# Gate and up projections of a SwiGLU layer in seven block products instead of eight

## The chip, the core and the metric

The kernel runs on one core of a Trainium2 chip. The measure is device microseconds of one execution, lower is better. The kernel before was timed three times: 1968.71, 1971.62 and 1972.38 us, with a median of 1971.62 us.

Five engines work side by side: TensorE (PE) multiplies, VectorE (DVE), ScalarE (ACT) and GpSimd (POOL) do elementwise work, and SyncE (SP) issues most of the transfers between main memory and on-chip memory (SBUF). PE writes only into PSUM, an accumulator memory that is used here as eight banks of 128 x 512 floats. Each engine works its instructions in a fixed order and waits at an instruction until what it needs is there.

## The reference

Two layers, each an attention block A and then a feed-forward block B, over 2048 rows of width 512, all in float32. The change touches only B:

```python
x = x + _A_ref(_layernorm(x), ...)
x = x + _B_ref(_layernorm(x), B_w_gate, B_w_up, B_w_down)
...
def _B_ref(x, w_gate, w_up, w_down):      # 512 x 1792, 512 x 1792, 1792 x 512
    g = _silu(x @ w_gate)
    u = x @ w_up
    return (g * u) @ w_down
```

A is causal attention of 32 heads of 16 in four segments of 512 rows, with a running memory (M, z) that is carried from segment to segment, and an output projection.

## The kernel before

**Precision by splitting.** Every float32 operand of a projection is split into a high part in PE's faster format (an ACT copy that rounds) and a low part, the rest (a subtraction on DVE, in attention partly on POOL). A product is three groups of matmuls: high x high, low x high, high x low. So one 512-deep product of a 128 x 512 tile is 3 x 4 = 12 matmuls with 512 columns each, and a 256-deep one is 6.

**The feed-forward stage** (`ffn`, line 799). The 1792 hidden columns are cut into 7 chunks of 256 (`NF`), the rows into 4 blocks of 512. A loop over chunks holds a loop over the blocks. For a chunk and a block, `up` (line 846) makes two halves of 128 columns; each is a gate product and an up product of 12 matmuls into their own banks (line 856), a silu on ACT (line 865), the product of both on DVE (line 866), and the split into high and low h (lines 868 and 869). `down` (line 874) then makes four products of 6 matmuls with `w_down` (line 883), and DVE adds each to the block's running result in SBUF (line 888). Weights are fetched once per chunk by `load_gu` and `load_d`; `load_part` (line 808) copies the high part on ACT (814) and makes the low part on DVE (815). All four blocks' normed and transposed rows stay in SBUF for the whole stage (buffers `H0` to `H3`, `L0` to `L3`).

**What sets the order.** The kernel records all operations with a priority and a cost, and `Program.issue` (line 144) then lays them out: it walks an own model of the engines' time and gives each engine, whenever it is free, the ready operation of lowest priority number. Each engine's instruction order is fixed by that. Priorities are places on a time line, `base + v * T`: in the feed-forward stage v counts blocks. `EARLY_AT` lets the first two blocks of chunk 0 start inside attention's last segment.

**Buffers.** Big tiles take named slots (`ffn_slots`, `att1`, `att2`); a new tile in a slot waits for all operations of the one before. The PSUM banks are `plt_0` to `plt_2`, `ppv`, `pmx_0`, `pmx_1` and two `pj`. `up` takes the first four in turn, `down` the `pmx` and `pj` banks.

## Time and profile before

| | before |
|---|---|
| median of three runs | 1971.62 us |
| profiled execution: time, span | 1972.77 us, 1971.0 us |
| PE busy in the span, matmuls | 1925.4 us, 11392 |
| DVE, ACT, POOL busy | 1145.0, 733.3, 474.0 us |
| PE's granted clock | 0.997 of full |

The profile is one execution. A busy time is the sum of an engine's instructions; PE's is of overlapping, pipelined matmuls. A group of instructions is given by line, engine, operation and tiles, with its count, its busy time, the mean of one, and after the bar the engine's idle time just before it and what ended that. A window row gives the same for a stretch of the span. Line numbers are those of the kernel before; tile names `s` are SBUF slots.

### The profile page before, as it was taken

To read this page: it belongs to the slowest core of one execution; us is meant where nothing else is said; L and a number is where in the kernel's file an instruction comes from. 1 tells how busy PE (TensorE), PEld (TensorE's weight loads), DVE (VectorE), ACT (ScalarE), POOL (GpSimd) and SP (SyncE) were. 2 spreads that over 40 slices of the span, in tenths; PEclk is the share of its full clock that TensorE was granted. 3 is DMA by queue.
4 is the path that set the end of the run, shared out by engine and by line. 5 is a ranking of instruction groups with operands and counts; after the bars stand their busy time and mean duration, and the time that the engine had idled before them with its cause. 6 is when DMAs were issued, how large, how long until landed. Compare 5 with 4: busy or idle time off the path is not lost.

```text
span 1971.0 us, 31446 instructions
## 1 busy us (share of the span) xinstructions
PE 1925.4 (98%) x11392; PEld 1493.2 (76%) x11392; DVE 1145.0 (58%) x3446; ACT 733.3 (37%) x1374; POOL 474.0 (24%) x731
## 2 busy tenths in 40 slices
PE   7999999999999999999999999999989999999999
PEld 5677677776778888888877777777767788888887
DVE  5877777778653333333558777776885433333333
ACT  4555554545521221121235545454554221211211
POOL 5333444434310000000333344343343000000000
PEclk9999999999999999999999999999999999999999
DMA  7444434456230100010364344453552201100002
GB/s 236 130 114 129 125 118 146 132 153 194 81 107 12 32 22 27 16 33 22 102 203 114 114 143 116 119 156 119 177 156 98 74 12 32 33 22 11 17 1 86
DMA packets 101547, 184.01 MB, mean 93 GB/s; under 512 B 12816, under 2 KB 28176, under 8 KB 101392
## 3 DMA queue, kind: packets, MB, share of 16 engines
q1 hardware_dynamic: 99344, 181.47, 30.2%
q8 instruction: 91, 1.49, 0.3%
q10 hardware_dynamic: 2048, 0.53, 0.1%
q14 instruction: 64, 0.52, 0.1%
HBM read 114.32 MB, written 67.11 MB: 92 GB/s over the span
## 4 chain that ended last, share of the span: by engine, by line
PE 89%; DVE 3%; DMA 3%; ACT 2%; issue 1%; POOL 1%; SPq 0%; ACTq 0%; DVEq 0%; POOLq 0%
PE plt L856 22%; PE pj L278 16%; PE pmx L527 8%; PE pj L883 8%; PE pmx L883 8%; PE ppv L856 7%; PE ppv L599 7%; PE plt L571 6%; PE pj L856 2%; DVE junk L534 1%; DMA s<-nm 1%; DMA ck<-scrk 1%; PE pj L369 1%; PE pmx L278 1%; PE pj L649 1%
## 5 line engine op out<-in xcount | busy, mean ns | idle before, releaser
L856 PE MATMUL plt<-s,s 128*128 128x512 f32 x1872 | 536.6, 393 | 0.0
L534 DVE CUSTOM_DVE_ANT_0 junk<-pmx,amask 128x128 bf16<-128x128 f32 (+3 forms) x1024 | 458.5, 484 | 128.1 <-PE pmx L527 123.4
L278 PE MATMUL pj<-s,s 128*128 128x512 f32 x1416 | 476.6, 409 | 0.3
L856 PEld LDWEIGHTS plt<-s,s 128*128 128x128 f32 x1872 | 351.1, 188 | 79.6 <-issue 0.8
L577 ACT ACTIVATE s<-plt 128x512 f32<-128x512 f32 x512 | 284.3, 600 | 156.1 <-PE plt L571 139.5
L527 PE MATMUL pmx<-ck,s 127*128 127x256 f32 (+2 forms) x1024 | 301.7, 349 | 17.1 <-DVE mx L534 10.8
L278 PEld LDWEIGHTS pj<-s,s 128*128 128x128 f32 x1416 | 263.0, 190 | 65.4 <-issue 24.5
L571 PE MATMUL plt<-s,ck 128*128 128x256 f32 x1280 | 242.7, 289 | 7.6 <-DMA s<-nm 6.2
L527 PEld LDWEIGHTS pmx<-ck,s 127*128 127x128 f32 x1024 | 179.5, 190 | 91.8 <-DVE mx L534 29.0
L856 PE MATMUL ppv<-s,s 128*128 128x512 f32 x624 | 243.9, 392 | 0.0
L571 PEld LDWEIGHTS plt<-s,ck 128*128 128x128 f32 x1280 | 214.0, 191 | 35.2 <-DMA s<-nm 7.9
L883 PE MATMUL pj<-s,vt 128*128 128x512 f32 x696 | 177.0, 393 | 0.0
L581 POOL TENSOR_SCALAR_AFFINE_SELECT s<-s 128x512 f32<-128x512 f32 x192 | 127.2, 665 | 194.9 <-ACT s L577 180.4
L865 ACT ACTIVATE Y<-plt 128x512 f32<-128x512 f32 x52 | 31.1, 598 | 370.8 <-PE plt L856 370.8
L883 PE MATMUL pmx<-s,vt 128*128 128x512 f32 x648 | 161.3, 394 | 1.0 <-ACT vt L868 1.0
L866 DVE TENSOR_TENSOR Y<-Y,plt 128x512 f32<-128x512 f32 x52 | 35.7, 687 | 214.6 <-ACT Y L865 214.6
L883 PEld LDWEIGHTS pj<-s,vt 128*128 128x128 f32 x696 | 130.8, 188 | 30.1 <-DVE s L374 0.3
L883 PEld LDWEIGHTS pmx<-s,vt 128*128 128x128 f32 x648 | 121.6, 188 | 29.4 <-ACT vt L868 1.5
L856 PEld LDWEIGHTS ppv<-s,s 128*128 128x128 f32 x624 | 117.1, 188 | 26.5
L599 PE MATMUL ppv<-s,vt 128*32 128x512 f32 (+2 forms) x1536 | 136.8, 458 | 0.0
L866 DVE TENSOR_TENSOR raw<-raw,ppv 128x512 f32<-128x512 f32 x52 | 35.7, 687 | 170.4 <-ACT raw L865 169.6
L351 POOL TENSOR_SCALAR bmv<-bmv 128x1 f32<-128x1 f32 x64 | 16.7, 263 | 490.2 <-DVE bmv L350 486.2
(130 smaller groups left out, 2087.4 us busy)
## 6 DMA issues: line engine op xcount, KB each, us to landing
s<-scrq SPq DMA_DIRECT2D x128, 192.0 KB, 3.5
ck<-scrk SPq DMA_DIRECT2D x128, 192.0 KB, 4.4
scrq<-s SPq DMA_DIRECT2D x32, 512.0 KB, 2.9
scrk<-s SPq DMA_DIRECT2D x32, 512.0 KB, 3.2
scrq<-s SPq DMA_DIRECT2D x32, 256.0 KB, 2.0
scrk<-s SPq DMA_DIRECT2D x32, 256.0 KB, 2.0
xin<-xmid SPq DMA_DIRECT2D x32, 256.0 KB, 2.7
s<-xmid SPq DMA_DIRECT2D x32, 256.0 KB, 4.7
```

The costliest lines, as they stand in the source:

```text
L278: pe(n, passes, lambda: nc.tensor.matmul(view(ps.ap), lhsT=av(a.ap), rhs=bv(b.ap), start=start, stop=stop), [(a, rk[0]), (b, rk[1])], [ps])
L369: pe(128, 2, lambda kc=kc: nc.tensor.transpose(ps.ap[:, kc * 128:(kc + 1) * 128], xn.ap[:, kc * 128:(kc + 1) * 128], ident.ap), [xn, ident ...
L527: nc.tensor.matmul(ps.ap[:, a * 256:a * 256 + nk], lhsT=cq.ap[0:127, 2 * j + p, qt * 128:(qt + 1) * 128], rhs=ck.ap[0:127, p, 0:nk], start ...
L534: dve(w, lambda a=a, qt=qt, w=w, ps=ps, junk=junk: nc.vector.tensor_tensor_reduce(out=junk.ap[:, :w], in0=ps.ap[:, a * 256:a * 256 + w], i ...
L571: nc.tensor.matmul(ps.ap[:, 256 * p:256 * p + 256], lhsT=ck.ap[:, p, kt * 128:kt * 128 + 128], rhs=cq.ap.rearrange("r (j p) c -> r p j c", ...
L577: act(512, lambda: nc.scalar.activation(Pb.ap[:, x].rearrange("p i c -> p (i c)"), ps.ap, AF.Exp, scale=SCALE), [ps], [(Pb, x)], table="exp")
L581: gp(0.593, lambda: nc.gpsimd.affine_select(out=Pb.ap[:, x], in_=Pb.ap[:, x], pattern=[[0, 4], [1, 128]], compare_op=OP.is_ge, fill=0.0, b ...
L599: nc.tensor.matmul(ps.ap[32 * i:32 * i + 32, q0:q0 + w], lhsT=vt.ap[:, kt, VW * hd:VW * hd + 32], rhs=f_[sl].ap[:, b0:b0 + w // 128, idx], ...
L856: pe(512, 1, lambda i=i, j=j, kc=kc, x=x, ps=ps, wt=wt: nc.tensor.matmul(ps.ap, lhsT=wt.ap[:, i, kc, cs], rhs=XT[b][j].ap[:, :, kc], start ...
L865: act(512, lambda: nc.scalar.activation(sg.ap, pg.ap, AF.Silu), [pg], [sg], table="silu")
L866: dve(512, lambda: nc.vector.tensor_mul(sg.ap, sg.ap, pu.ap), [sg, pu], [sg])
L883: pe(512, 1, lambda i=i, j=j, fi=fi, x=x, ps=ps, wt=wt, cs=cs: nc.tensor.matmul(ps.ap, lhsT=ht.ap[:, 0:2048].rearrange("p (f a c) -> p f a ...
```

## The change

**Seven products for eight.** Gate and up of chunks 1 to 6 are now computed for two blocks at once by `strassen` (new line 974). The 256 columns of a chunk are two halves of 128, the depth of 512 is two halves of 256, and the two blocks are the two columns of a 2 x 2 block product. The form has 7 products of 6 matmuls, with 7 additions on the result side, in place of 8 products of 6. Chunk 0 is done as before (`up`).

**Sums of weights.** For each chunk and matrix `load_s` makes four sums of weight quarters on POOL (new line 853), ACT copies the high parts (865), and POOL makes the low parts (866). Before, two ACT copies and two DVE subtractions did that.

**Sums of rows.** Once per pair of blocks `make_t` makes four sums of the rows' halves (`t0` to `t3`), high and low, for both quarters of each half: 20 sums and 8 low parts on DVE (new lines 906 and 928), 8 copies on ACT (927).

**Combining.** A `strassen` call uses three banks, called PX, PY and PZ, twice, three times and twice; gate takes the `plt` banks, up takes `ppv` and the `pmx` banks. ACT copies the first product to SBUF (new line 1005), and DVE makes the seven additions, each of a bank and an SBUF tile (1003). Silu reads SBUF now. `finish` multiplies two SBUF tiles (946) and splits the result (948 and 949).

**Pairs of blocks.** The loop over chunks now runs twice, once for blocks 0 and 1 and once for blocks 2 and 3, so every weight is fetched and prepared twice, and the slots of the first pair's rows are used again by the second. `down` takes only the two `pj` banks. A step (one chunk of one pair) has 84 matmuls of gate and up and 48 of down.

**Other edits.** A fourth raw buffer, the slots of both stages, and the priority of the second layer's first weights (`WQ1`).

The diff, cut to its core:

```diff
--- before.py
+++ after.py
...
+PAIR, STEP, WAT, TAT = 13.0, 1.83, -2.5, (-1.0, -0.5)
+T3E = "dve"
+WQ1 = -6.0
...
+    RAW = ("phik_0", "phik_1", "phiq_0", "phiq_1")
...
+                    at(WQ1)
                     load_w("q", wq, RAW)
+                    at(-2)
...
+        def wset():
+            nset[0] += 1
+            return [slots[f"w{nset[0] % 2}{e}"] for e in "ab"]
...
+        def load_s(c, nm):
+
+            a, b = [sb(tag, [128, 4, 2, 2, 128], F32R) for tag in wset()]
...
+            (r0, v0), (r1, v1) = [load_raw(wsrc(w, c, kp), RAW) for kp in range(2)]
+            m = [sb(f"mem_{i}", [128, 2, 2, 128]) for i in range(2)]
...
+            def ew(f, out, x, y, reads, w_):
+                gp(0.65, lambda: getattr(nc.gpsimd, f)(out(), x(), y()), reads, [w_])
+            ew("tensor_add", S1, A[1], A[3], [r0, r1], (m[0], 1))
+            ew("tensor_sub", S2, S1, A[0], [r0, (m[0], 1)], (m[0], 0))
+            ew("tensor_sub", S3, A[0], A[1], [r0], (m[1], 0))
+            ew("tensor_sub", S4, A[2], S2, [r1, (m[0], 0)], (m[1], 1))
+            for wt, o0, o1, src, read in ((a, 0, 1, lambda: v0()[:, :, 0:128].rearrange("p k (o f) -> p o k f", o=1), r0),
+                                          (a, 1, 3, lambda: m[0].ap, m[0]),
+                                          (b, 0, 2, lambda: v1().rearrange("p k (o f) -> p o k f", o=2), r1),
+                                          (b, 2, 4, lambda: m[1].ap, m[1])):
+                n = 256 * (o1 - o0)
+                hi = lambda wt=wt, o0=o0, o1=o1: wt.ap[:, o0:o1, 0]
+                lo = lambda wt=wt, o0=o0, o1=o1: wt.ap[:, o0:o1, 1]
+                act(n, lambda hi=hi, src=src: nc.scalar.copy(hi(), src()), [read], [(wt, (o0, 0))], sbuf=True)
+                gp(n / 400, lambda hi=hi, lo=lo, src=src: nc.gpsimd.tensor_sub(lo(), src(), hi().bitcast(F32)),
+                   [read, (wt, (o0, 0))], [(wt, (o0, 1))])
...
+            XT[b] = (sb(slots[f"H{b % 2}"], TX, F32R), sb(slots[f"L{b % 2}"], TX, F32R))
...
+        def make_t(m):
+
+            (h0, l0), (h1, l1) = XT[2 * m], XT[2 * m + 1]
+            R = [sb(slots[f"t{k}"], [128, 2, 4, 2, 128], F32R) for k in range(4)]
+            TT.update(enumerate(R))
...
+            def one(kc):
+                half = lambda b, k: (b, lambda: b.ap[:, :, 2 * k + kc].bitcast(F32))
+                raws = {}
...
+                def diff(k, eng, tags, ha, la, a, hb, lb, b):
+                    d, r = tmp(tags[0]), tmp(tags[1])
+                    ew(eng, "tensor_sub", d, half(ha, a), half(hb, b))
+                    ew(eng, "tensor_sub", r, half(la, a), half(lb, b))
+                    ew(eng, "tensor_add", r, r, d)
+                    raws[k] = r
+
+                def less(k, tag, ha, la, a, j):
+                    r = raws[k] = tmp(tag)
+                    ew("dve", "tensor_sub", r, half(ha, a), raws[j])
+                    ew("dve", "tensor_add", r, r, half(la, a))
+
+                def spl(k):
+                    b, r = raws[k]
+                    hi, lo = [lambda a=a: R[k].ap[:, a, :, kc] for a in range(2)]
+                    act(512, lambda: nc.scalar.copy(hi(), r()), [b], [(R[k], (0, kc))], sbuf=True)
+                    dve(512, lambda: nc.vector.tensor_sub(lo(), r(), hi().bitcast(F32)),
+                        [b, (R[k], (0, kc))], [(R[k], (1, kc))])
+                diff(2, T3E, ("xn_2", "xn_3"), h1, l1, 1, h1, l1, 0)
+                diff(0, "dve", ("tt_0", "tt_1"), h1, l1, 0, h0, l0, 0)
+                less(1, "of", h1, l1, 1, 0)
+                spl(0)
+                less(3, "tt_0", h0, l0, 1, 1)
+                for k in (1, 3, 2):
+                    spl(k)
+            one(0)
+            one(1)
+
...
+        def finish(sg, sv, ht, fi, pu, ru):
+            dve(512, lambda: nc.vector.tensor_mul(sv(), sv(), pu()), [sg, ru], [sg])
...
+        def strassen(c, nm, m, hts=None, sgs=None):
+
+            a, b = Wg[c, nm]
+            (h0, l0), (h1, l1) = XT[2 * m], XT[2 * m + 1]
+            PX, PY, PZ = [bank(t) for t in (("plt_0", "plt_1", "plt_2") if nm == "g" else ("ppv", "pmx_0", "pmx_1"))]
+            C = {}
+            for e, t in zip(((0, 0), (0, 1), (1, 0), (1, 1)),
+                            ("tt_0", "tt_1", "of", "raw") if nm == "g" else ("Y", "xn_2", "xn_3", "pc")):
+                C[e] = sb(t, [128, 2 if t == "pc" else 1, 512])
+
+            def prod(ps, w, o, xop):
+                key = (0 if w is a and o == 0 else 1 if w is a else 0 if o < 2 else 2)
+                seq = [(i, j, kc) for i, j in ((0, 0), (1, 0), (0, 1)) for kc in range(2)]
+                for x, (i, j, kc) in enumerate(seq):
+                    buf, view, rk = xop[j]
+                    rk = (rk, kc) if rk is not None else None
+                    pe(512, 1, lambda i=i, kc=kc, x=x, buf=buf, view=view: nc.tensor.matmul(
+                        ps.ap, lhsT=w.ap[:, o, i, kc], rhs=view(buf.ap, kc), start=(x == 0),
+                        stop=(x == len(seq) - 1)), [(w, (key, i)), (buf, rk)], [ps])
...
+            prod(PX, a, 0, blk(h0, l0, 0))
+            act(512, lambda: nc.scalar.copy(C[0, 0].ap[:, 0], PX.ap), [PX], [C[0, 0]])
+            prod(PY, a, 1, tk(1))
+            add(C[0, 1], PY, C[0, 0])
+            prod(PZ, b, 0, blk(h0, l0, 1))
+            add(C[0, 0], PZ, C[0, 0])
+            prod(PY, b, 2, tk(2))
+            add(C[1, 0], PY, C[0, 1])
+            prod(PX, a, 2, tk(0))
+            add(C[1, 1], PX, C[1, 0])
+            add(C[0, 1], PX, C[0, 1])
+            prod(PZ, b, 1, tk(3))
+            add(C[1, 0], PZ, C[1, 0])
+            prod(PY, b, 3, blk(h1, l1, 1))
+            add(C[0, 1], PY, C[0, 1])
+            order = ((0, 0), (1, 1), (1, 0), (0, 1))
+            if nm == "g":
+                for e in order:
+                    gate(C[e], lambda e=e: C[e].ap[:, 0], lambda e=e: C[e].ap[:, 0], C[e])
+                return C
+            for e in order:
+                finish(sgs[e], lambda e=e: sgs[e].ap[:, 0], hts[e[1]], e[0], lambda e=e: C[e].ap[:, 0], C[e])
...
+                ps = bank("pj")
...
+        for m in range(2):
+            v = m * PAIR
+            if m:
+                at(v - 3.0)
+                load_gu(RAW)
+                load_d(0, RAW)
+                for b in (2, 3):
...
                     ln(b)
...
+                at(v - 0.66)
+                down(NF - 1, 0, hts[0])
+                at(v + 0.33)
+                down(NF - 1, 1, hts[1])
+                for b in range(2):
+                    hts[b] = hbuf(1 - b)
+                    for fi in range(2):
+                        at(v + b + 0.5 * fi)
+                        up(b + 2, fi, hts[b], False)
+            at(v + TAT[m])
+            make_t(m)
+            pend = (0, 1) if m else (1,)
+            for c in range(1, NF):
+                v = m * PAIR + 2 + (c - 1) * STEP
+                at(v + WAT)
+                load_s(c, "g")
+                load_s(c, "u")
+                load_d(c, RAW)
+                at(v)
+                sgs = strassen(c, "g", m)
+                end = m == 1 and c == NF - 1 and not isinstance(x_out, Buf)
+                before = hts
+                for part in ("ud" if end else "du"):
+                    at(v + (0.6 if part == "d" and not end else 1.2))
+                    if part == "d":
+                        for b in pend:
+                            down(c - 1, b + 2 * m, before[b])
+                    else:
+                        hts = {b: sb(slots[f"X{b}"], [128, 4 * 512], F32R) if end else hbuf(1 - b) for b in range(2)}
+                        strassen(c, "u", m, hts, sgs)
+                pend = (0, 1)
+        v = 2 * PAIR
+        at(v)
+        for b in range(2):
+            down(NF - 1, b + 2, hts[b])
+        P.base = base + (v + 0.5) * T
...
+    ffn_slots = dict(H0="s1", L0="s2", H1="s4", L1="s5", w1a="s6", w1b="s7", w0a="s16", w0b="s17", d0="s0", d1="s8",
+                     X0="s3", X1="s10", X2="s9", X3="s11", t0="s14", t1="s15", t2="s12", t3="s13", h0="vt0", h1="vt1")
```

How it moves instructions, at the places that matter. In the names, `pj`, `plt`, `ppv`, `pmx` are PSUM banks, `vt` holds the split h, `Y`, `raw`, `tt`, `of`, `xn`, `pc` are SBUF tiles of one 128 x 512 block, `phik` and `phiq` raw weights, `mem` sums of weights, and `s` slots.

**DVE in the first layer, from one chunk to the next.** Before, the end of a block's up and its outputs:

```order
L866 TENSOR_TENSOR Y<-Y,plt_8702 128x512 [waits PE_49,Activation_49]
L869 TENSOR_TENSOR vt_8738<-Y,vt_8738 128x512 [waits Activation_49]
L866 TENSOR_TENSOR raw<-raw,ppv 128x512 [waits PE_49,Activation_49]
L869 TENSOR_TENSOR vt_8738<-raw,vt_8738 128x512 [waits Activation_49]
L888 TENSOR_TENSOR s_6516<-s_6516,pmx_8761 128x512 [waits PE_49]
L888 TENSOR_TENSOR s_6516<-s_6516,pmx_8763 128x512 [waits PE_49]
L888 TENSOR_TENSOR s_6516<-s_6516,pj_8779 128x512 [waits PE_49]
L888 TENSOR_TENSOR s_6516<-s_6516,pj_8781 128x512 [waits PE_49]
```

Now, the same place at the end of chunk 3's up (`pmx_8275`, `pmx_8307` and `ppv` are its banks, `plt_8379` and `plt_8390` those of chunk 4's gate):

```order
L1003 TENSOR_TENSOR pc<-ppv,xn_8341 128x512 [waits DVE_49,PE_49]
L1003 TENSOR_TENSOR xn_8309<-ppv,xn_8309 128x512
L1003 TENSOR_TENSOR xn_8341<-pmx_8307,xn_8341 128x512 [waits DVE_49,PE_49]
L946 TENSOR_TENSOR raw<-raw,pc 128x512
L946 TENSOR_TENSOR of<-of,xn_8341 128x512 [waits DVE_49]
L1003 TENSOR_TENSOR xn_8309<-pmx_8275,xn_8309 128x512 [waits PE_49]
L949 TENSOR_TENSOR vt_8377<-raw,vt_8377 128x512 [waits Activation_49]
L946 TENSOR_TENSOR tt_8173<-tt_8173,xn_8309 128x512 [waits DVE_49]
L949 TENSOR_TENSOR vt_8344<-of,vt_8344 128x512 [waits Activation_49]
L949 TENSOR_TENSOR vt_8377<-tt_8173,vt_8377 128x512 [waits Activation_49]
L1003 TENSOR_TENSOR tt_8416<-plt_8379,tt_8398 128x512 [waits DVE_49,PE_49]
L1003 TENSOR_TENSOR tt_8398<-plt_8390,tt_8398 128x512 [waits DVE_49,PE_49]
```

Six operations on two SBUF tiles (946 and 949), two of them before up's last addition and four behind it, now stand ahead of the addition that empties `plt_8379`.

**PE at that place,** now: the last rows before the matmul of chunk 4's gate that waits for that addition (the last one below). From the last matmul of up's last product to it there are 22 others, of which 11 are shown.

```order
L990 MATMUL plt_8379<-s_7265,s_8187 128x512
L990 MATMUL plt_8390<-s_6355,s_8233 128x512
L990 MATMUL plt_8364<-s_7221,s_8187 128x512 [waits Activation_49]
L990 MATMUL plt_8390<-s_6366,s_8233 128x512
L990 MATMUL plt_8364<-s_7221,s_8187 128x512
L990 MATMUL plt_8390<-s_6366,s_8233 128x512
L990 MATMUL plt_8364<-s_7221,s_8187 128x512
L1036 MATMUL pj_8418<-s_8068,vt_8344 128x512
L990 MATMUL plt_8364<-s_7221,s_8187 128x512
L1036 MATMUL pj_8418<-s_8068,vt_8344 128x512
L990 MATMUL plt_8364<-s_7221,s_8187 128x512
L990 MATMUL plt_8379<-s_7500,s_8233 128x512 [waits DVE_49]
```

Before, up's banks took turns in four with outputs between, and no bank was used twice within a product.

**POOL at that place,** now (before, POOL had nothing in this stage): the low parts of chunk 4's up weights, and the first sums of chunk 5's gate.

```order
L866 TENSOR_TENSOR s_8351<-phiq_8082,s_8351 128x256 [waits Activation_49]
L866 TENSOR_TENSOR s_8351<-mem_8219,s_8351 128x2x256 [waits Activation_49]
L866 TENSOR_TENSOR s_8383<-phiq_8086,s_8383 128x2x256 [waits Activation_49]
L866 TENSOR_TENSOR s_8383<-mem_8262,s_8383 128x2x256 [waits Activation_49]
L853 TENSOR_TENSOR mem_8414<-phiq_8366 128x256 [waits DMAHW7_49,Pool_49]
L853 TENSOR_TENSOR mem_8432<-phiq_8366,phiq_8405 128x256 [waits DMAHW0_49]
```

The first two follow up's fifth product, the next two its seventh, since those are the last readers of the two weight tiles.

**DVE at the end of the first layer's attention.** Before, after the last head's transpose:

```order
L612 STREAM_TRANSPOSE tt_7200<-ppv 128x512 [waits PE_49]
L613 RECIPROCAL r_7209<-tt_7200 128x16 [waits DVE_49]
L614 TENSOR_SCALAR r_7209<-r_7209,gnot 128x16 [waits DVE_49]
L616 TENSOR_TENSOR Y<-tt_7200,r_7209 128x16x16 [waits DVE_49]
L629 STREAM_TRANSPOSE of<-Y 128x512 [waits DVE_49]
L631 TENSOR_TENSOR of<-of,pj_7205 128x512 [waits DVE_49,PE_49]
L696 TENSOR_TENSOR xn_6111<-xn_6111,pmx_6900 128x512 [waits PE_49]
L696 TENSOR_TENSOR xn_6131<-xn_6131,pmx_6991 128x512 [waits PE_49]
L866 TENSOR_TENSOR raw<-raw,pj_7250 128x512 [waits PE_49,Activation_49]
L888 TENSOR_TENSOR s_6272<-s_6272,pj_7232 128x512 [waits PE_49]
```

Now:

```order
L615 STREAM_TRANSPOSE tt_7178<-ppv 128x512 [waits PE_49]
L616 RECIPROCAL r_7186<-tt_7178 128x16 [waits DVE_49]
L617 TENSOR_SCALAR r_7186<-r_7186,gnot 128x16 [waits DVE_49]
L619 TENSOR_TENSOR Y<-tt_7178,r_7186 128x16x16 [waits DVE_49]
L906 TENSOR_TENSOR tt_7198<-s_6976,s_6366 128x512 [waits DVE_49]
L632 STREAM_TRANSPOSE of<-Y 128x512
L906 TENSOR_TENSOR tt_7198<-tt_7198,tt_7085 128x512 [waits DVE_49]
L634 TENSOR_TENSOR of<-of,pj_7182 128x512 [waits DVE_49,PE_49]
L928 TENSOR_TENSOR s_7221<-tt_7198,s_7221 128x4x128 [waits DMAHW4_49,DMAHW2_49,Activation_49]
L906 TENSOR_TENSOR of<-s_6963,tt_7198 128x512 [waits Pool_49]
L906 TENSOR_TENSOR of<-of,s_6976 128x512 [waits DVE_49]
L906 TENSOR_TENSOR tt_7262<-s_6976,s_6366 128x512
```

The norms and transposes of blocks 2 and 3 are gone from here, and the sums of rows stand between the last head's operations and the output additions.

154 lines of the change are left out of this document (81 added, 73 removed).

## Prediction

> **What bounds the kernel now.** I read the page's busy times first, then the chain of waits, then the feed-forward stage by itself.
>
> The busy times and the chain that ended last, from the page:
>
> ```profile
> span 1971.0 us, 31446 instructions
> PE 1925.4 (98%) x11392; PEld 1493.2 (76%) x11392; DVE 1145.0 (58%) x3446; ACT 733.3 (37%) x1374; POOL 474.0 (24%) x731
> ...
> PE 89%; DVE 3%; DMA 3%; ACT 2%; issue 1%; POOL 1%; SPq 0%; ACTq 0%; DVEq 0%; POOLq 0%
> ```
>
> PE is busy for 98% of the span and is 89% of the chain. In two long stretches inside the feed-forward stages (columns: window, length, busy time and count of PE, PEld, DVE, ACT, POOL) nothing else comes near it:
>
> ```profile
> 600.00:900.00 300.00, 300.00 (x1303) 244.50 (x1302) 111.66 (x172) 58.26 (x99) 0.00 (x0) 1.00 0.08 23
> 1550.00:1900.00 350.00, 350.00 (x1520) 285.23 (x1519) 129.02 (x198) 67.22 (x114) 0.00 (x0) 1.00 0.07 21
> ```
>
> PE never stops, at full clock; DVE is busy 37% of the time, ACT 19%, POOL not at all. One matmul takes 350.00 / 1520 = 0.230 us of PE. So a matmul less in this stage is 0.230 us less, as long as PE still never waits.
>
> **The change part by part.**
>
> *Removed.* The gate and up matmuls stand in three groups, by bank:
>
> ```profile
> L856 PE MATMUL plt<-s,s 128*128 128x512 f32 x1872 | 536.6, 393 | 0.0
> ...
> L856 PE MATMUL ppv<-s,s 128*128 128x512 f32 x624 | 243.9, 392 | 0.0
> ...
> L856 PE MATMUL pj<-s,s 128*128 128x512 f32 x192 | 66.2, 419 | 0.2
> ```
>
> That is 2688. The changed program issues 384 of the old form (chunk 0) and 48 calls of `strassen` with 7 products of 6 matmuls, 2016, together 2400. The 288 that go are worth 288 x 0.230 = **66.2 us**, certain as work and lost only where PE now waits.
>
> *Added on DVE.* 336 combining adds and 112 operations of `make_t`, less 12 weight splits. One step (one chunk, two blocks) has 32 DVE rows: 14 adds from PSUM, 4 products, 4 splits of h, 8 output adds, 2 splits of `w_down`. Two adds back to back, and one split of each kind:
>
> ```profile
> 700.70 1.28 DVE L888 TENSOR_TENSOR s<-s,pmx 128x512 f32<-128x512 f32 x2
> ...
> L815 DVE TENSOR_TENSOR s<-phik,s x41: 680/683/692, 605.1 to 1846.2; 128x512 fp32r<-128x512 f32 x41
> L868 ACT CAST vt<-raw 128x512 fp32r<-128x512 f32 x60 | 37.2, 620 | 39.4 <-DVE raw L866 33.8 <-PE pj L883 5.6
> ```
>
> One DVE operation lasts 0.68, and the next follows 1.28 - 0.68 = 0.60 us after its start. A step is 32 x 0.60 = 19.2 us of DVE against 132 x 0.230 = 30.4 us of PE: 63%, so as a sum DVE does not bound. ACT's 20 rows a step at up to 0.62 are 12.4 us, and the 84 more loads of 256 KB meet DMA engines that are busy 7 to 8% in the rows above. These cost nothing while PE has 30 us a step; without that cover the adds alone would cost 14 x 0.60 = 8.4 us a step.
>
> *Added on POOL: a lock.* POOL, idle in this stage before, now does 16 operations a step (8 sums of weights, 8 splits). Its splits are two-input operations on SBUF like line 467, 1.288 us each; the quarter-size ones have no row and lie between a 128x1 operation and the full one:
>
> ```profile
> L467 POOL TENSOR_TENSOR s<-raw,s x64: 1260/1288/1609, 22.1 to 1436.2; 128x512 fp32r<-128x512 f32 x64
> ...
> L351 POOL TENSOR_SCALAR bmv<-bmv 128x1 f32<-128x1 f32 x64 | 16.7, 263 | 490.2 <-DVE bmv L350 486.2
> ```
>
> I take 0.7 (nearest the half of 1.288). What such an operation does to DVE shows at the start of the kernel, first DVE, then POOL:
>
> ```profile
> 21.81 2.40 DVE L424 TENSOR_TENSOR s<-s,s 128x512 fp32r<-128x512 f32 x2 [2.69 <-ACT s L417]
> ...
> 24.44 3.39 DVE L424 TENSOR_TENSOR s<-s,s 128x512 fp32r<-128x512 f32 x3
> ```
>
> ```profile
> 22.08 1.58 POOL L467 TENSOR_TENSOR s<-raw,s 128x512 fp32r<-128x512 f32 x1
> ...
> 25.07 1.61 POOL L467 TENSOR_TENSOR s<-raw,s 128x512 fp32r<-128x512 f32 x1
> ```
>
> Two DVE operations that read both operands from SBUF take 2.40 us, not 1.28; POOL's takes 1.58, not 1.29. They exclude each other: POOL waits 0.3 us for the DVE operation under way, then the DVE operation behind it waits until POOL ends at 23.66 and is done 0.55 us later (21.81 + 2.40 = 24.21). So in a run of both kinds they alternate. Operations with one operand in PSUM are not held:
>
> ```profile
> L374 DVE TENSOR_TENSOR s<-pj,s 128x512 fp32r<-128x512 f32 x60 | 40.2, 682 | 9.6 <-ACT s L373 9.1
> ```
>
> These 60 run among attention's POOL work at a mean of 682 ns. The Trainium skill, "SBUF — State Buffer", section "Who interferes with whom", says so: a DVE instruction with two SBUF inputs contends with a GpSimd instruction that reads SBUF, one with at most one does not. The trace agrees (2.40 against 682 ns).
>
> *Where it hits.* The order rows show the place: the end of an up product. There DVE has, in order, product of element (1,1), product of (1,0), the last add, a split, the product of (0,1), two splits, and then the add that empties the gate's second bank for the next step. PE has 22 matmuls from the end of up's last product to the matmul that waits for that add: 22 x 0.230 = 5.06 us. And there POOL splits up's next weights, since their slot comes free with up's last products. My ledger for the place shown, in us from the last up matmul, hand-overs of 0.2 from PE taken in (an estimate: the rows show a matmul lasting 0.39 with 0.23 between starts, so its result is 0.16 late):
>
> - Up's sixth product ends 5 matmuls earlier, at -1.15. Its add starts at -0.95; the two products at -0.35 and 0.25, the last add at 0.86, the split of (1,1) at 1.46, ending 2.15.
> - ACT: cast of (1,1) to 0.95, cast of the weights to 1.57. POOL's first full split starts at 1.7, waits for DVE's split to 2.15 and ends at 3.44.
> - The product of (0,1), ready at 2.07, waits to 3.44 and ends at 4.0. POOL's second split then runs to 5.29. The split of (1,0) waits for it, ends at 5.85; the last split ends at 6.45 and the gate's add at 7.06.
> - PE gets it near 7.1. Without the lock: (0,1) at 2.07, cast to 3.4, split to 4.1, add to 4.7, 0.36 us before PE wants it.
>
> Over the 20 step boundaries (five in each of four pairs) the order leaves PE 20 to 28 matmuls, 22.8 on average, 5.24 us. The stall is 7.1 - 5.24 = 1.9 us, so 20 x 1.9 = **38 us**. Bounds: 0, if DVE keeps its turn; 7.1 + 0.7 - 5.24 = 2.5 us, 50 us in all, if POOL's next weight sum slips in as well. I take 1.9, since both pairs above alternate. Behind the held DVE row stand all of the next gate's adds, which PE's banks wait for; what is late next is that whole gate, so the stall is not caught up.
>
> *`make_t` at four pair starts.* 28 DVE operations, 28 x 0.60 = 16.8 us, nearly all with both operands in SBUF. At attention's end they go where DVE is fullest:
>
> ```profile
> 450.00:500.00 50.00, 44.81 (x337) 32.07 (x336) 44.59 (x176) 27.02 (x51) 24.64 (x40) 1.00 0.59 170
> 500.00:550.00 50.00, 49.00 (x285) 36.82 (x285) 26.56 (x58) 22.01 (x40) 18.99 (x31) 1.00 0.26 85
> ```
>
> They begin in the second window, where DVE has 23.4 us free, and PE has 58 matmuls (13.3 us) between the last attention product and the first that needs a sum. But POOL's order there has six weight sums and one split, 6 x 0.7 + 1.3 = 5.5 us, in the same place. Bounds: 0, if the cover holds, and 5.5, if every POOL operation is paid in full; the middle, 3 us at each of four starts, is **12 us** (0 to 22).
>
> *Moved.* Blocks 0 and 1 are finished half a stage early, so the second layer's rows are there sooner. At that start PE now idles 3.8 us:
>
> ```profile
> 1000.00:1050.00 50.00, 46.21 (x274) 34.10 (x273) 31.23 (x121) 20.65 (x39) 15.54 (x22) 0.97 0.51 161
> ```
>
> I count 0 (bound: 3.8 gained), since the work that starts there still follows the last output adds of the stage in PE's order. SP's queue issues 84 more loads, with a priority 2.5 blocks ahead of their use; behind a load that is held stand the rows for the norm of blocks 2 and 3, which the 5.5 us at a pair start bound.
>
> *Sum* against the profiled execution, 1972.77 us (span 1971.0 and 1.8 around it): 1972.8 - 66.2 + 38 + 12 = 1956.6. That execution is 1.15 us above the median of the three runs, 1971.62, so **1955 us**.
>
> **The rivals.**
>
> - *The lock does not reach PE.* The groups fall apart in time, or DVE's turn comes first. Then 1972.8 - 66.2 - 1.2 = 1905, some leftover at the pair starts makes it 1908. For: the ledger has 0.36 us to spare without the lock. Against: POOL's splits and DVE's are released by the same up product, so they meet at every boundary.
> - *`make_t` is exposed: slower.* At a pair start the sums form a chain (the T for product 2 needs the one for product 5), and PE runs in fixed order, so it stands at the first matmul that needs one. If 10 of the 16.8 us are bare at each of four starts in place of 3, it is 4 x 7 = 28 us more: 1983. It decides from 3 + 16.2/4 = 7 us a start on. For: DVE is at 44.59 of 50 before it. Against: 13.3 us of other matmuls lie ahead of it on PE.
> - *DVE's ping-pong with PE.* Up's second bank is emptied in 6 matmuls, 1.38 us, for a wait of 0.2 and an add of 0.68. If another DVE operation is under way each time, 0.6 us too late 48 times, 1955 + 29 = 1984. Against: the output adds there come from banks that PE fills itself, one per 1.38 us. I give it no chance of its own but let the range hold it.
>
> **How the numbers follow.** Forecast (the lock costs most of the gain) 0.5, with its own range 1930 to 1972; lock not felt 0.24; `make_t` or the ping-pong bare 0.26. About 0.2%, 3.9 us, is what a measurement can tell from no change. Of the forecast's 0.5, 0.43 are faster by more than that, 0.06 within it, 0.01 slower. With the first rival's 0.24, faster is 0.67; with 0.03 of the last case, the same is 0.09; its other 0.23 make slower 0.24. The range, 1912 to 1985, leaves about 0.1 on each side: the fully gained 66 us below, several mishaps above.
>
> **What would show it.** Right: about 288 fewer matmuls at 0.230; at each step boundary one PE idle of about 2 us before a matmul of the gate's second bank, released by DVE; DVE rows of the h splits and products well over 0.69 us, POOL splits over 1.29, adds from PSUM at 0.68. Wrong: PE at 100% in the middle of the stage (then the first rival), or PE idle mostly at the four pair starts, released by ACT or DVE rows of `make_t` (then the second). The sum is wrong altogether if a matmul of the new form takes other than 0.230 us.

## The result and the profile after

The changed kernel took 2032.6 us (median of four executions, 2027.3 to 2036.0), the kernel before 1972.0: a ratio of 1.031, 95% interval 1.028 to 1.034. It is **slower by 3%**; the forecast was 1955, faster by 0.9%, and the range ended at 1985. The 288 matmuls did go. What came in their place is in the page of the changed kernel:

```profile
span 2025.2 us, 32344 instructions
PE 1902.1 (94%) x11104; PEld 1443.2 (71%) x11104; DVE 1496.9 (74%) x3882; ACT 873.1 (43%) x1634; POOL 885.0 (44%) x1115
...
PE 33%; DVE 10%; issue 2%; POOL 1%; DMA 1%; ACT 1%; SPq 0%; DVEq 0%; ACTq 0%; POOLq 0%
```

PE has 11104 matmuls, 288 fewer than 11392, and is busy for 94% of the span in place of 98%. The last line is the chain that ended last. Its shares add up to only 48% of the span in this page, so its 33% of PE cannot be set beside the 89% of before; of what it covers, DVE has 10 of 48, before 3 of 99. The same two stretches of the feed-forward stages as in the prediction (window, length, busy time and count of PE, PEld, DVE, ACT, POOL, granted clock, DMA share, GB/s):

```profile
600.00:900.00 300.00, 275.15 (x1149) 216.94 (x1148) 215.73 (x317) 96.78 (x174) 140.29 (x142) 0.96 0.19 57
1550.00:1900.00 350.00, 323.93 (x1354) 254.64 (x1353) 256.17 (x359) 118.24 (x213) 165.19 (x158) 0.97 0.21 65
...
663.00:689.00 26.00, 26.00 (x114) 21.05 (x113) 17.90 (x28) 8.31 (x16) 9.29 (x10) 1.00 0.18 51
```

Two things are new. PE stands for 24.9 of the first 300 us, and the **granted clock** is 0.96, where it was 1.00. Between the stalls nothing is wrong: the third row is the middle of a step, PE full, 26.00 / 114 = 0.228 us a matmul, as before.

**A step boundary**, with the row order that the ledger of the prediction assumed: DVE, then POOL, then PE, in three timelines of the same place (start, duration, operation; the last matmul of up starts at 904.67).

```profile
905.89 0.68 DVE L1003 TENSOR_TENSOR xn<-pmx,xn 128x512 f32<-128x512 f32 x1
906.49 0.68 DVE L949 TENSOR_TENSOR vt<-raw,vt 128x512 fp32r<-128x512 f32 x1
907.09 1.78 DVE L946 TENSOR_TENSOR tt<-tt,xn 128x512 f32<-128x512 f32 x1
908.79 1.78 DVE L949 TENSOR_TENSOR vt<-of,vt 128x512 fp32r<-128x512 f32 x1
910.49 1.21 DVE L949 TENSOR_TENSOR vt<-tt,vt 128x512 fp32r<-128x512 f32 x1
911.80 1.49 DVE L1003 TENSOR_TENSOR tt<-plt,tt 128x512 f32<-128x512 f32 x2
```

```profile
906.62 1.70 POOL L866 TENSOR_TENSOR s<-phiq,s 128x512 fp32r<-128x512 f32 x1 [1.80 <-ACT s L865]
908.28 1.75 POOL L866 TENSOR_TENSOR s<-mem,s 128x512 fp32r<-128x512 f32 x1
910.10 1.05 POOL L853 TENSOR_TENSOR mem<-phiq 128x256 f32<-128x256 f32 x1
```

```profile
910.08 0.40 PE L990 MATMUL plt<-s,s 128*128 128x512 f32 x1
912.55 1.76 PE L990 MATMUL plt<-s,s 128*128 128x512 f32 x6 [2.07 <-DVE tt L1003]
```

The three DVE rows of 1.78, 1.78 and 1.21 us are 0.69 long when nothing holds them (685 ns in run 1). Each pairs with a POOL row that ends just before it does: 908.32 and 908.87, 910.03 and 910.57, 911.15 and 911.70. The gate's add ends at 911.80 + 0.68 = 912.48, and PE's next matmul starts at 912.55, after 2.07 us of waiting.

**The clock.** Two boundaries, each with the stretch of 3.4 us behind it (same columns as above):

```profile
656.00:659.40 3.40, 0.39 (x2) 0.00 (x0) 3.30 (x4) 0.62 (x1) 3.19 (x3) 1.00 0.10 35
659.40:662.80 3.40, 3.26 (x8) 2.58 (x9) 0.78 (x2) 1.44 (x3) 1.49 (x3) 0.52 0.00 0
690.20:693.60 3.40, 1.79 (x8) 1.12 (x6) 3.30 (x4) 0.62 (x1) 3.32 (x3) 1.00 0.24 77
693.60:697.00 3.40, 2.94 (x12) 2.28 (x13) 1.10 (x2) 0.93 (x2) 1.35 (x3) 1.00 0.02 5
```

After PE has stood for 3.0 of 3.4 us, the next 3.4 us run at half clock: 8 matmuls in 3.26 us, 0.41 each. After 1.6 us of standing nothing follows.

**The pair start** of the second pair: POOL's timeline, the first and the last of twelve DVE rows beside it with the row behind them, and PE's wait from the whole run's list of waits (total, times, longest):

```profile
793.22 7.75 POOL L866 TENSOR_TENSOR s<-phik,s 128x256 fp32r<-128x256 f32 x1 [15.06 <-ACT s L865]
```

```profile
793.07 0.68 DVE L906 TENSOR_TENSOR xn<-xn,xn 128x512 f32<-128x512 f32 x1
...
799.70 0.69 DVE L906 TENSOR_TENSOR tt<-tt,s 128x512 f32<-128x512 f32 x1
800.30 0.68 DVE L1041 TENSOR_TENSOR s<-s,pj 128x512 f32<-128x512 f32 x1
```

```profile
PE pmx L990 <- POOL s L866: 10.5, 4, 6.7
```

A quarter split, 0.74 us when alone, took 7.75: meanwhile DVE ran twelve operations of `make_t` and of weight splits back to back, all with two SBUF operands, and each lasted its normal 0.69. Here POOL is the one that is shut out, and PE stands 6.7 us for it. POOL's row ends at 800.97, beside the first DVE row that has an operand in PSUM.

### The profile page after: what moved, and what is told of

Read it like the earlier page. It is cut to its first block, busy times and chain, and to the rows that moved or that the text cites. A ratio compares the mean times of both kernels' runs of the same rounds, so it can differ in the third digit from the quotient of the medians.

```text
span 2025.2 us, 32344 instructions
## 1 busy us (share of the span) xinstructions
PE 1902.1 (94%) x11104; PEld 1443.2 (71%) x11104; DVE 1496.9 (74%) x3882; ACT 873.1 (43%) x1634; POOL 885.0 (44%) x1115
## 5 line engine op out<-in xcount | busy, mean ns | idle before, releaser
L1036 PE MATMUL pj<-s,vt 128*128 128x512 f32 x1296 | 408.4, 400 | 11.9 <-DVE s L1041 6.9
L990 PE MATMUL plt<-s,s 128*128 128x512 f32 x1008 | 321.6, 412 | 52.7 <-DVE tt L1003 35.9
L1036 PEld LDWEIGHTS pj<-s,vt 128*128 128x128 f32 x1296 | 245.0, 191 | 80.0 <-DVE s L1041 13.8
L990 PEld LDWEIGHTS plt<-s,s 128*128 128x128 f32 x1008 | 194.1, 196 | 116.3 <-DVE tt L1003 46.9
L990 PE MATMUL pmx<-s,s 128*128 128x512 f32 x720 | 249.4, 401 | 11.6 <-POOL s L866 10.5
L1041 DVE TENSOR_TENSOR s<-s,pj 128x512 f32<-128x512 f32 x224 | 152.6, 684 | 130.7 <-PE pj L1036 130.5
L574 PEld LDWEIGHTS plt<-s,ck 128*128 128x128 f32 x1280 | 213.9, 190 | 30.7 <-ACT s L580 5.0
L990 PEld LDWEIGHTS pmx<-s,s 128*128 128x128 f32 x720 | 137.2, 191 | 44.9 <-POOL s L866 12.2
L866 POOL TENSOR_TENSOR s<-phiq,s 128x256 fp32r<-128x256 f32 (+1 forms) x48 | 61.2, 1276 | 194.2 <-ACT s L865 194.2
L866 POOL TENSOR_TENSOR s<-phik,s 128x256 fp32r<-128x256 f32 (+1 forms) x48 | 59.5, 1241 | 193.1 <-ACT s L865 193.1
L866 POOL TENSOR_TENSOR s<-mem,s 128x512 fp32r<-128x512 f32 x96 | 138.8, 1447 | 1.9 <-ACT s L865 1.8
L990 PE MATMUL ppv<-s,s 128*128 128x512 f32 x288 | 113.2, 393 | 0.0
```

What stands on the lines that cost most here:

```text
L574: nc.tensor.matmul(ps.ap[:, 256 * p:256 * p + 256], lhsT=ck.ap[:, p, kt * 128:kt * 128 + 128], rhs=cq.ap.rearrange("r (j p) c -> r p j c", ...
L866: gp(n / 400, lambda hi=hi, lo=lo, src=src: nc.gpsimd.tensor_sub(lo(), src(), hi().bitcast(F32)), [read, (wt, (o0, 0))], [(wt, (o0, 1))])
L990: pe(512, 1, lambda i=i, kc=kc, x=x, buf=buf, view=view: nc.tensor.matmul(ps.ap, lhsT=w.ap[:, o, i, kc], rhs=view(buf.ap, kc), start=(x == 0),
L1036: pe(512, 1, lambda i=i, j=j, fi=fi, x=x, ps=ps, wt=wt, cs=cs: nc.tensor.matmul(ps.ap, lhsT=ht.ap[:, 0:2048].rearrange("p (f a c) -> p f a ...
L1041: dve(512, lambda ps=ps, t=t: nc.vector.tensor_add(xb.ap[:, t, :], xb.ap[:, t, :], ps.ap), [ps, (xb, t)], [(xb, t)])
```

## The experiments

The theory is that POOL's reads and DVE's two-operand reads of SBUF exclude each other (the prediction's lock), and that the stalls this causes also halve the clock. The rivals are DVE's order and the length of its chain, POOL's mere lateness, and Strassen's products themselves as cause of the clock. Times are medians; ratios are to the kernel before, run beside each.

**1. POOL writes but reads nothing.** In `load_s`:

```
-                gp(0.65, lambda: getattr(nc.gpsimd, f)(out(), x(), y()), reads, [w_])
+                gp(0.65, lambda: nc.gpsimd.memset(out(), 0.01), reads, [w_])
...
-                gp(n / 400, lambda hi=hi, lo=lo, src=src: nc.gpsimd.tensor_sub(lo(), src(), hi().bitcast(F32)),
+                gp(n / 400, lambda lo=lo: nc.gpsimd.memset(lo().bitcast(F32), 0.0),
```

> Edit: POOL's 8 weight sums and 8 weight splits of a step are replaced by memsets of the same tiles at the same place in POOL's order, so POOL writes SBUF there and reads nothing; left out are the weight sums and the low parts of the weights of chunks 1 to 6. The order of PE, DVE and ACT is the changed kernel's, row for row. Theory (the lock): the h splits and products fall from 1.2 to 1.8 us back to 0.69, the 20 step boundaries lose their stalls of 2.6 us (52 us), the half-clock spells that follow them go (about 20 us), and a POOL split can no longer be kept out by make_t's row of DVE operations, 6.9 us at one pair start: 1920 us, 1908 to 1940. Rival (the order itself: DVE's chain of product, cast, split and add is longer than the 22 matmuls also without POOL): stalls of 1 to 2 us stay at the boundaries, 1975 us or more. Rival (the half clock comes from the new matmuls, not from the stalls): the spells stay at about 50 us in the two feed-forward stages, 1945 us.

Measured: **1918.9 us**, ratio 0.973 (0.971 to 0.975), inside the theory's range. Its feed-forward windows, and two groups of its DVE rows:

```profile
600.00:900.00 300.00, 297.08 (x1295) 238.67 (x1294) 218.27 (x358) 110.80 (x201) 61.00 (x159) 1.00 0.21 65
```

```profile
L946 DVE TENSOR_TENSOR tt<-tt,xn 128x512 f32<-128x512 f32 x24 | 16.4, 685 | 0.0
L949 DVE TENSOR_TENSOR vt<-of,vt 128x512 fp32r<-128x512 f32 x23 | 15.8, 685 | 0.2
```

The same two groups in the changed kernel; in the two traces the rows of PE, DVE and ACT stand in the same order from the first to the last:

```profile
L946 DVE TENSOR_TENSOR tt<-tt,xn 128x512 f32<-128x512 f32 x24 | 38.8, 1616 | 0.0
L949 DVE TENSOR_TENSOR vt<-of,vt 128x512 fp32r<-128x512 f32 x23 | 29.3, 1273 | 0.0
```

1616 and 1273 ns become 685, the stalls at the boundaries are gone, and the clock is 1.00. The order and the chain alone cost next to nothing, so that rival is out; so is the one that makes the clock a matter of the new matmuls. A memset is also shorter than the work it replaces (474 ns in the mean for the splits), so this run takes away POOL's lateness together with its reads; runs 5 and 8 keep the work.

**2. Only the splits write.** The second line of that edit alone.

> Edit: only POOL's splits of the Strassen weights become memsets (left out are the low parts of the weights of chunks 1 to 6); the 8 sums of a step stay, which read two operands from SBUF and last 0.74 us when nothing holds them. The order is the changed kernel's on every engine. Theory (the lock, as my prediction had it, by the splits): a boundary loses the two splits of 1.45 us and keeps at most one or two sums of 0.74, so the stalls fall from 2.6 to under 1 us and no half clock follows: 1935 us, 1915 to 1960. Rival (the sums slip in at the boundary and hold DVE as much): 1980 to 2000 us, stalls of 1.5 to 2 us.

Measured: **1928.1 us**, 0.978 (0.976 to 0.980). The splits carry nearly all of it; the sums, which still read, cost 9 us. In the changed kernel's list of PE's waits, and then in this one's, the boundary is

```profile
PE plt L990 <- DVE tt L1003: 35.9, 16, 3.3
```

```profile
PE plt L990 <- DVE tt L1003: 2.8, 5, 0.7
```

2.8 us in 5 waits, against 35.9 in 16.

**3. The gate's add ahead of the last split.**

```
-                            ("tt_0", "tt_1", "of", "raw") if nm == "g" else ("Y", "xn_2", "xn_3", "pc")):
+                            (("tt_0", "tt_1", "of", "raw") if c % 2 else ("tt_0", "raw", "of", "tt_1")) if nm == "g" else ("Y", "xn_2", "xn_3", "pc")):
...
+            at(fin)
             for e in order:
                 finish(sgs[e], ...)
...
-                        strassen(c, "u", m, hts, sgs)
+                        strassen(c, "u", m, hts, sgs, v + STEP + 0.2)
```

> Edit: every second step the gate's sums for elements (0,1) and (1,1) swap their tiles, so that the gate's first add no longer writes the tile that the last h split of the step before still reads; and up's products and splits get a later priority, so that the gate's first add stands ahead of the last split in DVE's order. POOL's work is unchanged. Theory (lock plus DVE's order): one held split of 1.2 us leaves the chain ahead of the add at each of 20 boundaries, 24 us, and a stall of 1.4 us is too short for the half clock to follow, another 20 us: 1985 us, 1970 to 2000. Rival (the stall is POOL's or ACT's, and DVE's order does not matter): 2027 us, no change.

Measured: **2001.2 us**, 1.014 (1.013 to 1.016): 31 us better than the change, a microsecond outside the range, and still slower than before. DVE's timeline at one boundary:

```profile
859.65 1.79 DVE L946 TENSOR_TENSOR raw<-raw,xn 128x512 f32<-128x512 f32 x1
861.36 1.23 DVE L949 TENSOR_TENSOR vt<-tt,vt 128x512 fp32r<-128x512 f32 x1
862.51 1.21 DVE L949 TENSOR_TENSOR vt<-of,vt 128x512 fp32r<-128x512 f32 x1
863.65 0.68 DVE L1003 TENSOR_TENSOR tt<-plt,tt 128x512 f32<-128x512 f32 x1
```

The last split now stands behind the add (at 864.25); the three held rows shown, and one of 1.51 us before them, are left ahead of it. The stalls did not fall to the expected 1.4 us: most boundaries still have 2.1 to 2.6, and with them 37.5 us of half clock after 480 us, where the change has 61.4. The order decides how many held rows count; it does not make them short.

**4. POOL's work put later in the order only.** The list of what up's weight work depends on gets the gate's second add; the weight work of the next gate gets the add of the step before it. The planner places POOL's rows accordingly:

```
+            late = [o for o in P.ops[first:] if o.eng == "pool"]
+            late = [o for o in late if nm == "g" or o is not late[4]]
+            for o in late:
+                o.deps |= set(mark.get(c if nm == "u" else c - 1, ()))
...
+                mark[c] = P.ops[-1:]
...
```

> Edit: nothing is left out; POOL's weight work of a step (up's 8 sums and splits but for the first quarter split, and the next gate's) waits until DVE has done the gate's first two adds, so POOL reads nothing in the 5 us at the step boundary. Theory (the lock acts there and only there): the boundary stalls go to under 0.5 us, the spells with them, the pair starts keep their 15 to 25 us: 1930 us, 1915 to 1950. Rival (POOL's 17 us of a 30 us step are then late for the next weights, and PE waits on a POOL split instead): a stall of 2 us or more at up's or gate's first products, 1965 us or more.

Measured: **2032.8 us**, 1.030 (1.029 to 1.032), as the change. POOL's timeline at a boundary shows why:

```profile
652.58 0.74 POOL L869 TENSOR_TENSOR s<-phik,s 128x256 fp32r<-128x256 f32 x1 [10.78 <-ACT s L868]
653.28 0.74 POOL L856 TENSOR_TENSOR mem<-phik,phik 128x256 f32<-128x256 f32 x1
653.98 0.74 POOL L856 TENSOR_TENSOR mem<-phik 128x256 f32<-128x256 f32 x1
654.68 1.20 POOL L856 TENSOR_TENSOR mem<-mem,phik 128x256 f32<-128x256 f32 x1
656.52 1.30 POOL L869 TENSOR_TENSOR s<-phik,s 128x512 fp32r<-128x512 f32 x1 [0.65 <-ACT s L868]
657.78 1.18 POOL L856 TENSOR_TENSOR mem<-phik,mem 128x256 f32<-128x256 f32 x1
```

The dependency existed for the planner and not as a semaphore: no data goes from that add to POOL. With nothing ahead of it in its queue POOL ran as soon as the weights were there, at the same boundary, with six rows. So neither theory nor rival was tested: an order is not a wait.

**5. The same with a real wait.** POOL first reads a column that the add writes; the rest of the edit is that of run 4:

```
+                seen = sb("seen", [128, 1])
+                gp(0.2, lambda: nc.gpsimd.tensor_scalar(seen.ap, C[0, 0].ap[:, 0, 0:1], 1.0, 0.0, op0=OP.mult, op1=OP.add),
+                   [C[0, 0]], [seen])
...
```

> Edit: as in the run before this one POOL's weight work for up stands behind the gate's first two adds, but now by a real wait: POOL first reads one column of the gate's sum that DVE's second add writes, and up's sums and splits (all but the first quarter split) follow it in POOL's order. Nothing is left out. Theory (the lock at the boundary): with POOL silent there the h splits and products last 0.69 us and the stalls of 2 to 2.2 us go below 0.5: 1930 us, 1912 to 1955. Rival (POOL's work, 17 us of 30 a step, now comes late for up's first products or for the next gate's weights): PE waits for a POOL split for 2 us or more in most steps, 1965 us or more. Rival (the stall at the boundary is DVE's and ACT's own chain): 2020 us.

Measured: **1949.9 us**, 0.989 (0.987 to 0.991). All of POOL's work is there, at another time. DVE's groups:

```profile
L953 DVE TENSOR_TENSOR tt<-tt,xn 128x512 f32<-128x512 f32 x24 | 16.5, 688 | 0.5 <-ACT s L822 0.5
L956 DVE TENSOR_TENSOR vt<-of,vt 128x512 fp32r<-128x512 f32 x23 | 15.8, 689 | 0.3
```

688 and 689 ns, and the gate's add is not in this kernel's list of PE's waits at all. 83 us of 2033 come back when POOL is silent for the few us of each boundary. The planner laid out the other engines anew, so this trace does not keep the change's or run 4's order on PE, DVE and ACT as run 1 does; at a boundary looked at (612 to 619 us) DVE's rows from the product of (1,0) to the gate's add have the ledger's order, and each lasts 0.69. What is left against run 1 sits at the pair starts (one POOL split again takes 7.77 us there; stalls of 3.0 to 4.0 us) and at the first layer's end.

**6. Wait and order together** (edits 3 and 5).

> Edit: the wait of POOL together with the swapped tiles and the later priority of up's products, which let the gate's first add stand ahead of the last h split. Theory (lock): with POOL silent at the boundary DVE's order hardly matters: 1925 us, within 10 of the kernel with the wait alone. Rival (both are needed, because POOL's first quarter split and sums still meet DVE): 20 us or more below the kernel with the wait alone.

Measured: **1944.9 us**, 0.987 (0.985 to 0.989), 5 us below run 5: with POOL silent the order hardly matters, as the theory had it; the level is 20 above its 1925.

**7. and 8. The low parts of the weights on DVE**, so that POOL only sums; 8 with the order of run 3.

```
...
-                gp(n / 400, lambda hi=hi, lo=lo, src=src: nc.gpsimd.tensor_sub(lo(), src(), hi().bitcast(F32)),
-                   [read, (wt, (o0, 0))], [(wt, (o0, 1))])
+                was, P.prio = P.prio, P.prio + late * T
+                dve(n, lambda hi=hi, lo=lo, src=src: nc.vector.tensor_sub(lo(), src(), hi().bitcast(F32)),
+                    [read, (wt, (o0, 0))], [(wt, (o0, 1))])
+                P.prio = was
...
```

> Edit: the 8 low parts of a step's weights are made by DVE in place of POOL, with a priority behind up's work (gate's weights) and behind the gate's first adds (up's weights); POOL keeps the sums. Nothing is left out. Theory (lock): the kernel without POOL's splits took 1928 us; DVE gets 8 rows of 0.3 to 0.6 us more, 4 us a step to its 19, which PE's 30 us still cover: 1935 us, 1920 to 1960. Rival (DVE, 80% busy, answers PE's banks late): stalls of 0.5 us and more before the output products and up's second bank, 1970 us or more.

> Edit: the low parts of the weights on DVE, with the swapped tiles and the later priority of up's products. Nothing is left out. Theory (lock): the boundary has only POOL's sums to meet, and the gate's add no longer waits for the last split: 1930 us, 1915 to 1955, below the changed kernel and below the kernel before. Rival (DVE's load is the bound by now): 1970 us or more.

Measured: **1944.7 us**, 0.986 (0.984 to 0.987), and **1942.1 us**, 0.985 (0.983 to 0.987). Both are in the theory's ranges: the same splits cost less on the busier DVE than on a POOL that shuts DVE out, and DVE's load is not the bound yet.

**9. and 10. Earlier sums at the pair starts**, on runs 6 and 8:

```
-PAIR, STEP, WAT, TAT = 13.0, 1.83, -2.5, (-1.0, -0.5)
+PAIR, STEP, WAT, TAT = 13.0, 1.83, -2.5, (-2.0, -1.5)
...
-                        strassen(c, "u", m, hts, sgs, v + STEP + 0.2)
+                        strassen(c, "u", m, hts, sgs, v + (0.9 if m and c == NF - 1 else STEP + 0.2))
```

> Edit: the kernel with POOL's wait and the swapped tiles, with make_t's priority one block earlier in both pairs, and up's products of the layer's last chunk back at their earlier priority. Nothing is left out. What is left there by the trace is at the pair starts (stalls of 3.3 and 3.8 us before the gate's fourth product, which waits for a sum of make_t) and at the stage's end (3.4 us, the output products wait for the last h split), and two or three spells behind them. Theory: these 10 us and some 7 us of half clock go: 1930 us, 1920 to 1942. Rival (make_t only changes places with attention's last DVE work, which PE waits for then): 1945 us.

> Edit: the kernel with the weights' low parts on DVE and the swapped tiles, with the same two changes of priority. Theory: as there, 1932 us, 1920 to 1942; rival (DVE is full at the pair starts, an earlier make_t holds the output adds): 1942 us or more.

Measured: 1945.5 us (0.987, 0.985 to 0.989) and 1945.0 us (0.988, 0.986 to 0.990). No gain, the rival's outcome. In run 9's trace the wait for `make_t`'s cast at the first start is still 3.0 us, a new one of 2.0 us stands before it (for attention's last additions, line 699, on DVE), and at the stage's end 3.8 us are left where 3.2 were.

**11. Only up's low parts on DVE** (`if nm == "g"` keeps the POOL line for the gate's weights), with the order of run 3.

> Edit: the low parts of up's weights on DVE, those of the gate's weights on POOL as in the changed kernel, with the swapped tiles and up's products at the later priority. Nothing is left out. The gate's weights are split in the middle of a step, where DVE mostly adds from PSUM, so POOL's reads hold little there; the boundary has only DVE's splits. Theory (the lock costs only where DVE's row is the one that PE waits for): as with all the splits on DVE but with 2 us a step less for DVE, 1935 us, 1925 to 1945. Rival (POOL's gate splits run on into the boundary or starve at the pair starts): stalls of 2 us return there, 1955 us or more.

Measured: **1934.7 us**, 0.981 (0.979 to 0.983), the best of the complete kernels: 1.9% faster than before, 98 us below the change. Its feed-forward windows:

```profile
600.00:900.00 300.00, 297.25 (x1284) 239.45 (x1283) 233.86 (x387) 108.81 (x198) 102.17 (x121) 0.99 0.22 64
1550.00:1900.00 350.00, 346.40 (x1507) 279.33 (x1507) 268.62 (x435) 127.59 (x233) 115.48 (x131) 1.00 0.19 56
```

POOL still makes half of the splits and all sums, but only 19 of DVE's two-input rows of 128x512 last over 0.85 us (500 to 1030 and 1550 to 2010 us), where the change has 110: in the middle of a step, where DVE mostly adds from PSUM, POOL's work meets few rows that it can hold. That a held row which PE does not wait for costs nothing was not tested by itself.

**12 to 14. Stalls of a set length in the kernel before**, which has no Strassen product and no POOL work in the stage. DVE works on up's bank 4, 6 or 3 times (runs 12, 13 and 14), and PE's next gate product begins with one matmul on the outcome:

```
+            if c and not fi:
+                tl, tw = sb("tt_0", [128, 128], F32R), sb("tt_1", [128, 512])
+                for i in range(4):
+                    op("dve", 0.001, lambda: nc.vector.tensor_scalar_mul(tw.ap, pu.ap, 0.5), [pu], [tw])
+                op("dve", 0.001, lambda: nc.vector.tensor_copy(tl.ap, tw.ap[:, 0:128]), [tw], [tl])
+                hold_pe.append(tl)
...
```

> Edit to the kernel before (no Strassen, no POOL work in the stage): at 48 places in chunks 1 to 6, after an up product, DVE makes 4 operations of 0.6 us on up's bank and a small cast, and PE's next gate product begins with one 128x128 matmul that reads the cast's tile (its sum is overwritten, nothing is left out). So PE stands for about 1.4 us, 48 times. In the trace of the changed kernel the half-clock spells begin on a grid of 3.413 us, and they follow windows of that grid in which PE idled 1.94 us or more; of the windows with 1.0 to 1.87 us of idling only one was followed. Theory (the clock halves after a window with over half of it idle): stalls of 1.4 us leave the clock at 1.00 in the stage, time 1972 + 48 x 1.4 = 2040 us. Rival (any stall, or Strassen's mixture of work, brings it): spells as in the changed kernel, 25 us more or, without Strassen, none with the longer stall either.

> The same edit with 6 DVE operations in place of 4: stalls of about 2.6 us, 48 times. Theory: a stall of 2.6 us fills 1.9 us of one window for (2.6 - 0.4) / 3.41 = 65% of its positions on the grid, so about 31 spells of 3.41 us, 1.7 us lost in each: 1972 + 48 x 2.6 + 31 x 1.7 = 2150 us. Rival (the spells belong to Strassen's products): 2097 us and no spells in the stage.

> The edit with the inserted stalls once more, with 3 DVE operations. With 4 of them the 42 stalls in the steady part were 2.3 us each in place of the 1.4 expected, with 6 they were 3.5, so 0.6 an operation: 1.7 us each with 3, some 1.55 us of idling, which is below 1.9 us in any window. Theory (the clock halves only behind a window of the 3.413 us grid with 1.9 us or more of idling): granted clock 1.00 in the feed-forward stages and 1972 + 42 x 1.7 = 2043 us, some 10 more for the stalls at the stage's two ends. With 4 operations it was 2129. Rival (a stall costs half clock in proportion to its length): 1972 + 42 x 1.7 x (36 + 97) / 97 = 2070 us with about 15 spells.

Measured: 2067.4 us with 3 operations (1.049, 1.046 to 1.052), 2129.0 with 4 (1.080, 1.077 to 1.083), 2238.6 with 6 (1.136, 1.133 to 1.139). The absolute numbers missed in all three: with 4 the stalls came out 0.9 us longer than I had counted, with 6 likewise, and beside the stalls the edit costs some 19 us of its own. Run 14's time is even its rival's, 2070, but by way of those 19 us: the rival's 15 spells of half clock are not there. PE's wait for the inserted cast (total, times, longest) and the clock in the stage tell the lengths apart; with 3:

```profile
PE plt L857 <- DVE tt L873: 77.3, 47, 1.7
```

```profile
590.00:1015.00 425.00, 387.24 (x1668) 309.24 (x1667) 192.78 (x320) 74.42 (x126) 6.46 (x12) 1.00 0.10 28
```

with 4:

```profile
PE plt L857 <- DVE tt L873: 99.3, 46, 2.2
```

```profile
590.00:1015.00 425.00, 377.55 (x1565) 300.57 (x1564) 193.14 (x315) 70.95 (x120) 0.00 (x0) 0.96 0.07 22
```

with 6:

```profile
PE plt L857 <- DVE tt L873: 160.8, 48, 3.4
```

```profile
590.00:1015.00 425.00, 360.80 (x1397) 286.01 (x1396) 194.50 (x311) 61.28 (x103) 0.00 (x0) 0.90 0.06 17
```

Waits of 77.3 / 47 = 1.64 us leave the clock at 1.00; of 2.16 us bring it to 0.96, of 3.35 us to 0.90. DVE, which makes the stalls, is busy for 192.8, 193.1 and 194.5 us of the three stretches, so its load does not tell them apart. In the profiled executions (2069.2, 2125.5, 2235.8 against 1972.8) what goes beyond the waits is 19.1, 53.4 and 102.2 us. The half-clock spells from 500 us to the last matmul sum to 0, 75.1 and 204.8 us in the traces' record of the clock; half of that, 38 and 102, is the most they can cost, and by estimate, with 19.1 as the edit's own cost in all three, 53.4 - 19.1 = 34 and 102.2 - 19.1 = 83 is what they cost (part of the long ones lies in the stalls themselves). Run 13's way of counting, with the waits as they came out, gives (2.16 - 0.4) / 3.41 = 52% of 46, or 24 spells, and 87% of 48, or 42; the traces have 22 and 40, some of run 13's two windows long. Strassen has no part in it, and the cost is not in proportion to the stall: 1.64 us are free of it, 2.16 us are not.

## Why the prediction was wrong

Step by step, by the profiled executions (1972.8 before, 2027.3 after). "Gaps" are sums over the starts of successive matmuls in the trace, what exceeds 0.23 us, where it is 0.5 or more.

- **The removed matmuls**: right. 288 fewer, 0.228 us each in the new form at full clock; 66 us were there to be had, and run 1 got 49 of them.
- **The mechanism at the boundary**: right, to the row. The ledger, counted from 904.90, where the last up matmul has its 0.23 us behind it, had POOL's first full split end at 3.44 (measured 3.42), the product of (0,1) at 4.0 (3.97), the second split at 5.29 (5.13), the split of (1,0) at 5.85 (5.67), the gate's add at 7.06 (7.58). At the place that the prediction shows, the end of chunk 3's up at 686.40, the product ends at 3.98, the split at 5.68 and the add at 7.61.
- **Its size**: wrong, **the term of 38 us** is too small. The 20 boundaries have 53.5 us of gaps, 2.7 each in place of 1.9, beyond even the upper bound of 50. The ledger stopped at two POOL splits; on the chip one or two sums of 1.05 to 1.2 us slipped in behind them (the bound had one of 0.7), and DVE had three held rows at the place shown and four at some others, that at 656 us among them, where the ledger has two. In some steps PE was caught twice, since ACT's copy out of the gate's first bank stands behind casts that wait for the held rows (11 waits for that copy, 13.9 us in all).
- **`make_t`**: wrong, **3 us at each of four starts**. Starts and ends of the stage have 34.9 us of gaps, 11.9 of which run 1 has too. The other 23 are not DVE's work laid bare, as the second rival had it, for run 1 has all of that work in the same order. 10.5 of them are the lock the other way round, the waits for a POOL split shown above: DVE's unbroken run shuts POOL out for 7.75 us where the bound of 5.5 had counted POOL's own durations. The other 12 or 13 go with POOL's reads as well, but were not traced to single rows.
- **The step that was missing**: a stall also costs **half clock behind it**. Between 480 us and the last matmul the changed kernel has 61.4 us of half-clock spells, run 1 has none. Half of that is 30.7 us, less half of the 9.4 in which PE stood anyway: an estimate of 26 us, with no term in the sum. Runs 12 to 14 show it without Strassen.
- Together 53.5 + 23 + 26 = 102.5, and the changed kernel's profiled execution is 2027.3 - 1923.5 = 103.8 us above that of run 1, which differs in POOL's rows alone. The 17 us that run 1 still lies above 1972.8 - 66.2 = 1906.6 were not taken apart. So the forecast's miss, 2027.3 - 1956.6 = 70.7 us, is by these estimates 15.5 for the boundaries, 11 for the starts, 26 for the clock and 17 that stay open, with 1 left over.
- **The rivals**: none was right. That the lock does not reach PE is refuted by runs 1, 2 and 5. The ping-pong of up's second bank did not show: no wait of up's `ppv` or `pmx` matmuls for one of DVE's adds stands in PE's list.
- **The chances**: 0.67 for faster rested on a sum whose stall term had an upper bound that was one place's ledger, and on a stall priced by its own length.
